# A fused attention and channel-mix kernel whose written-out order is replaced, with the drawn numbers packed one unit to a partition and the last output cut 384 and 128

## The chip, the core and the metric

One core of one Trainium2 chip runs the whole kernel. Its engines are TensorE (PE; its weight loads are shown apart as PEld), VectorE (DVE), ScalarE (ACT) and GpSimd (POOL); SyncE (SP) issues every DMA of this kernel. Each engine takes its instructions in the order in which they were written. The metric is device microseconds of one execution, as the median of timed runs. The profile is one further execution.

## The reference

```python
def _attn_ref(q, k, v, sampled_blocks):
    B, H, S, D = q.shape                      # 4, 8, 768, 64
    block = 32
    n_blocks = S // block                     # 24
    scores = 1.0 / np.sqrt(D) * np.matmul(q, k.transpose(0, 1, 3, 2))
    # kept: neighbours within one block, the first and the last block (as row and as column),
    # and three drawn blocks for each block of rows
    ...
    for qb in range(n_blocks):
        for kb in sampled_blocks[qb]:
            mask[qb * block:(qb + 1) * block, kb * block:(kb + 1) * block] = True
    scores = np.where(mask, scores, -1000000000.0)
    attn = np.exp(scores - np.max(scores, axis=-1, keepdims=True))
    attn = attn / (np.sum(attn, axis=-1, keepdims=True) + 1e-09)
    return np.matmul(attn, v)

def _moe_ref(x, mu_k, mu_r, w_k, w_v, w_r):   # x is the attention's output, 4 x 768 x 512
    x_prev = np.concatenate([np.zeros((B, 1, D)), x[:, :-1, :]], axis=1)
    xk = mu_k * x + (1.0 - mu_k) * x_prev
    xr = mu_r * x + (1.0 - mu_r) * x_prev
    k = np.maximum(xk @ w_k, 0.0)             # 512 to 1024
    v = k * k @ w_v                           # 1024 to 512
    r = 1.0 / (1.0 + np.exp(-(xr @ w_r)))
    return r * v
```

The weights come as float64; queries, keys and values as float32.

## The kernel before, in words

The attention is cut into 26 units. Units u0 to u21 each hold one block of 32 rows of all four batches; block n of unit u(n-1) looks at eight blocks of keys: itself, its two neighbours, the first, the last and three drawn ones. Units u22 to u25 hold the first and the last block of one batch, which look at all keys. Of a unit, two halves of `scores` (PE, line 402; tile `s`) are followed by `top` (DVE, the row maximum), `less` and four `exp` on ACT, a transposition (up to u3 on PE as `turn` and a copy `turned`; from u4 on DVE with a DMA called `move`), `values` (PE, lines 436 and 475; tile `o`), a division on DVE, and a copy into the mixer's input (`turn x`, `put x`).

The mixer works on tiles of 256 rows in the order 1 to 10, 0, 11. Tile t needs three units of attention. It computes `xr` and `xk` (mixes of x with its shifted self, each split into a high and a low part), two gates `r{t}_0` and `r{t}_1` (line 716), four pairs of hidden products `h{t}_0` to `h{t}_3` (line 737) and the outputs `v{t}_i` (line 772). Every product is three matmuls of fp32r parts. DVE multiplies gate and output, and SP stores them.

The twenty weights (w0 to w3 of the gate, w4 to w11 of the hidden products, w12 to w19 of the outputs) are loaded raw (512 KB each, `raw`) and turned into the two fp32r parts by six operations each: `size` on ACT, `tail`, `sign` and `lo` on one of two or three engines, `join` on DVE and `hi` on ACT or POOL. `CHOICE` says which engine.

Keys sit in twelve slots of the tile `KA`, values in `VA`. The slot for the neighbour key of a unit is the one that the unit before has last read: `u5 keys` can be issued by SP only when both `scores` of u4 have ended, and whatever stands behind it on SP waits with it. Which blocks were drawn is known only at run time: `pack` on DVE puts six drawn numbers of a unit into one word of the tile `packed`, SP loads a word of it (`TENSOR_LOAD`, line 266) ahead of a unit's first drawn load and takes the block numbers out by shifts.

All 2139 operations are written into a list, and a table of numbers, `ORDER`, says in which order they are emitted; an engine executes its own operations in that order. 128 small matmuls called `warm` come first on PE.

Of the kernel before, what the change touches and what calls it, by code (L numbers as in the profile page):

```python
# [95 lines left out]
def block_sparse_attention_channel_mix(  # L96
# [31 lines left out]
    packed = fixed([1, NEARS], I32, "packed")  # L128
# [3 lines left out]
    def mask_setup():  # L132
        pairs = NEARS * NRAND * SAME_AS
        drawn = buf([1, 2, pairs, 2], I32, "x0", 1, "drawn")
        e = buf([1, NEARS, NRAND, SAME_AS], F32, "x1", 1, "equal")
        r = buf([1, 6, NEARS, NRAND], F32, "kk", 3, "pickf")
        plan.add("drawn", SP, ISSUE, lambda: nc.sync.dma_start(drawn.ap.rearrange("p a b c -> p (a b c)"), blocks), writes=[(drawn,)], size=60000)

        def pack():
# [10 lines left out]
            half = r.ap[:, 2:4, :, 0]  # L150
            v.scalar_tensor_tensor(out=half, in0=both[:, :, :, 2], scalar=float(ROOM), in1=both[:, :, :, 1], op0=ALU.mult, op1=ALU.add)
            v.scalar_tensor_tensor(out=half, in0=half, scalar=float(ROOM), in1=both[:, :, :, 0], op0=ALU.mult, op1=ALU.add)
            whole = r.ap[:, 4:6, :, 0].bitcast(I32)
# [609 lines left out]
    def values(t, i, k2, z, last):  # L763
        final = t == TILES[-1] and i == 1
        width = DM // 2 if final else DM
        for n in range(0, DM, width):
# [3 lines left out]
            def mm(f, pv=pv, cs=cs):  # L770
# [224 lines left out]
```

## Time and profile before

| what | value |
| --- | --- |
| median of three timed runs | 520.68 us (516.51 to 520.86) |
| profiled execution, its own time | 519.15 us |
| its span, first to last instruction | 517.4 us |
| PE busy | 487.2 us (94%) |
| DVE, ACT, POOL busy | 321.1, 306.3, 207.1 us (62, 59, 40%) |
| mean granted clock of TensorE | 0.97 |
| bytes moved by DMA | 114.65 MB |

A busy share is an average over the whole span; which engine sets the pace has to be read stage by stage. The profiled execution lies 1.75 us above its span and 1.53 us under the median of the timed runs.

### The profile page before, as it was taken

How to read it: one execution, taken by the hardware profiler on the slowest of the kernel's cores; microseconds unless marked ns; L12 is line 12 of the kernel's file. 1: busy time of each engine (PE TensorE's matmuls, PEld its weight loads, DVE VectorE, ACT ScalarE, POOL GpSimd, SP SyncE). 2: the span in 40 equal slices, each digit the busy share in tenths (PEclk: the TensorE clock that was granted, in tenths of full speed). 3: DMA queues.
4: the chain of work that ended last, by engine and by line, in shares of the span. 5: the costliest groups of instructions: out<-in, count | busy, mean ns of one | idle time of the engine just before them, and what ended most of it. 6: DMA issues, size and time to landing. Idle time of an engine off the chain costs nothing.

```text
span 517.4 us, 18098 instructions
## 1 busy us (share of the span) xinstructions
PE 487.2 (94%) x7384; PEld 402.9 (78%) x7384; DVE 321.1 (62%) x608; ACT 306.3 (59%) x701; POOL 207.1 (40%) x253
## 2 busy tenths in 40 slices
PE   4568798999999999999999999999999999999997
PEld 4245587778779888878778878868778879889896
DVE  3667797976775865765665766763765653434231
ACT  2886887875736755546664745664646564445441
POOL 2425454352611722253452442233543525434531
PEclk8678899999999999999999999999999999999999
DMA  8999999988978888888898889999669553100101
GB/s 267 383 336 303 347 312 300 294 237 227 287 240 260 253 224 253 224 275 224 228 270 231 256 248 263 278 261 355 201 144 315 161 135 86 38 22 20 42 22 41
DMA packets 58052, 114.65 MB, mean 222 GB/s; under 512 B 7665, under 2 KB 20721, under 8 KB 55026
## 3 DMA queue, kind: packets, MB, share of 16 engines
q1 hardware_dynamic: 57970, 113.50, 72.1%
q8 instruction: 58, 0.95, 0.8%
q14 instruction: 24, 0.20, 0.1%
HBM read 77.82 MB, written 6.29 MB: 163 GB/s over the span
## 4 chain that ended last, share of the span: by engine, by line
PE 68%; DMA 11%; SPq 8%; DVE 4%; issue 4%; ACT 2%; POOL 2%; DVEq 0%; POOLq 0%; ACTq 0%
PE v L772 18%; PE s L402 7%; PE h_0p L737 6%; PE h_1p L737 6%; PE r_0p L716 6%; PE h_2p L737 6%; PE h_3p L737 5%; PE r_1p L716 5%; DMA KA<-kt 4%; PE o L475 4%; PE o L538 2%; DMA KA<-kq 2%; SPq L463 2%; PE sw L496 2%; DMA pt<-r 2%
## 5 line engine op out<-in xcount | busy, mean ns | idle before, releaser
L772 PE MATMUL v<-w,k 128*128 128x512 f32 (+1 forms) x600 | 138.9, 385 | 0.0
L772 PEld LDWEIGHTS v<-w,k 128*128 128x128 f32 x600 | 107.9, 188 | 26.7 <-issue 5.0
L412 DVE TENSOR_REDUCE nm<-s 128x4 f32<-128x1024 f32 x44 | 53.0, 1214 | 18.6 <-PE s L402 17.5
L402 PE MATMUL s<-KA,q 64*32 64x256 f32 x1408 | 51.9, 428 | 12.9 <-DMA raw<-w_k 9.9
L452 ACT ACTIVATE p<-s,nm 128x256 f32<-128x256 f32 x144 | 60.7, 479 | 0.6
L402 PEld LDWEIGHTS s<-KA,q 64*32 64x32 f32 x1408 | 28.1, 118 | 29.3 <-issue 10.6
L455 DVE STREAM_TRANSPOSE r<-p 128x1024 f32<-128x1024 f32 x36 | 43.5, 1227 | 9.7 <-ACT p L452 8.0
L475 PEld LDWEIGHTS o<-VA,pt 128*32 128x32 f32 x2304 | 34.0, 109 | 7.7 <-issue 4.1
L475 PE MATMUL o<-VA,pt 128*32 128x65 f32 x2304 | 37.4, 221 | 1.9 <-DMA pt<-r 1.1
L737 PE MATMUL h_2p<-xk,w 128*128 128x256 f32 x288 | 38.1, 285 | 0.2 <-ACT h_0k L752 0.2
L737 PEld LDWEIGHTS h_2p<-xk,w 128*128 128x128 f32 x288 | 36.0, 192 | 2.3 <-issue 1.2
L737 PEld LDWEIGHTS h_0p<-xk,w 128*128 128x128 f32 x288 | 35.6, 189 | 2.5 <-issue 1.0
L737 PEld LDWEIGHTS h_3p<-xk,w 128*128 128x128 f32 x288 | 35.6, 190 | 2.4 <-issue 1.2
L737 PE MATMUL h_3p<-xk,w 128*128 128x256 f32 x288 | 37.4, 285 | 0.0
L737 PE MATMUL h_0p<-xk,w 128*128 128x256 f32 x288 | 37.0, 282 | 0.4 <-DVE z L778 0.4
L716 PE MATMUL r_1p<-w,xr 128*128 128x512 f32 x144 | 37.2, 399 | 0.0
L737 PE MATMUL h_1p<-xk,w 128*128 128x256 f32 x288 | 37.1, 283 | 0.0
L737 PEld LDWEIGHTS h_1p<-xk,w 128*128 128x128 f32 x288 | 35.3, 189 | 1.5 <-issue 0.8
L716 PE MATMUL r_0p<-w,xr 128*128 128x512 f32 x144 | 36.5, 399 | 0.0
L666 ACT ACTIVATE xr_0d<-xt,mk 128x128 f32<-128x128 f32 x48 | 19.3, 402 | 21.3 <-DVE xr_0f L673 15.2
L716 PEld LDWEIGHTS r_0p<-w,xr 128*128 128x128 f32 x144 | 26.2, 188 | 6.7 <-issue 0.8
L416 ACT ACTIVATE nm<-nm 128x4 f32<-128x4 f32 x44 | 8.9, 202 | 36.1 <-DVE nm L412 36.0
(237 smaller groups left out, 837.7 us busy)
## 6 DMA issues: line engine op xcount, KB each, us to landing
VA<-vt SPq DMA_DIRECT2D x92, 260.0 KB, 4.5
KA<-kt SPq DMA_DIRECT2D x89, 256.0 KB, 4.3
pt<-r SPq DMA_DIRECT2D x72, 256.0 KB, 4.9
VA<-vw SPq DMA_DIRECT2D x24, 260.0 KB, 5.4
KA<-kq SPq DMA_DIRECT2D x16, 384.0 KB, 5.5
ptw<-rw SPq DMA_DIRECT2D x32, 192.0 KB, 3.6
out<-z SPq DMA_DIRECT2D x23, 256.0 KB, 3.7
q<-qt SPq DMA_DIRECT2D x22, 256.0 KB, 4.5
```

What stands on the lines that cost most here:

```text
L402: nc.tensor.matmul(s.ap[ROWS[j], row, a * 256 : (a + 1) * 256].rearrange("p (n x) -> p n x", x=BLK), q.ap[half, (hp * QB + j) * BLK : (hp ...
L412: nc.vector.tensor_reduce(out=nm.ap.rearrange("p (r a) -> p r a", r=2), in_=s.ap.rearrange("p r (a x) -> p r a x", a=2), axis=AX.X, op=ALU ...
L452: plan.add(f"u{name} exp {i}", ACT, 365, lambda row=row, a=a, i=i: nc.scalar.activation(squares()[:, :, :, i, :], s.ap[:, row, a * 256 : ( ...
L455: plan.add(f"u{name} turn", DVE, N_TURN, lambda: nc.vector.transpose(out=r.ap[:, :, gi].rearrange("p j c i x -> p j (c i x)"), in_=squares ...
L463: nc.sync.dma_start(pt.ap[:, b].rearrange("p g c i x -> p (g c i x)"), r.ap[ROWS[b]].rearrange("p j g c i x -> p j (g c i x)"))
L475: nc.tensor.matmul(o[gi].ap[ROWS[j], i * DV : (i + 1) * DV], pt.ap[:, j, gi, g, 2 * row + a, :], VA.ap[:, c0 + g, j, h * DV : (h + 1) * DV ...
L496: nc.tensor.matmul(s.ap[HALF[a], row, 0:W], q.ap[half, 2 * hp * BLK : 2 * (hp + 1) * BLK], wide_keys(b, hp)[half, k * W : (k + 1) * W], st ...
L538: nc.tensor.matmul(o.ap[ROWS[2 * a + e], c * DV : (c + 1) * DV], pt.ap[:, 2 * a + e, row, n, :], VA.ap[:, c1, part, h * DV : (h + 1) * DV] ...
L666: nc.scalar.activation(parts(d.ap), cols(c, 0), AF.Copy, scale=mk.ap[:, which, c : c + 1])
L716: nc.tensor.matmul(pr.ap[:, 0:512], xr.ap[:, a, c, :], weight_of["r", c].ap[:, w, :], start=(c == 0 and m == 0), stop=(c == CC - 1 and m = ...
L737: nc.tensor.matmul(ph.ap[:, ff * TT : (ff + 1) * TT], weight_of["k", c, f2 // 2].ap[:, w, f % 4 * P : (f % 4 + 1) * P], xk.ap[:, a, c, :], ...
L772: nc.tensor.matmul(pv.ap[:, 0:width], k2.ap[:, a, f, i * P : (i + 1) * P], weight_of["v", f].ap[:, w, cs], start=(f == 0 and m == 0), stop ...
```

## The change

Four edits are made.

1. `pack` works on 22 partitions, one unit each, in place of one partition: nine instructions as before, each over 1/22 of the elements. The drawn numbers are loaded as 22 rows of 336 bytes, and SP reads the word of a unit from that unit's partition.
2. The last output of the last tile, 512 columns, was computed in two parts of 256 columns; now in one of 384 and one of 128.
3. `ORDER` is replaced, and with it `CHOICE`: 18 in place of 14 `put x` of the attention's units run on ACT, 27 in place of 22 `hi` of xr on POOL, 23 in place of 16 `lo` of xr on DVE, and some others move one for one.
4. `warm` can take a data type. Its choice stays number 6, 128 matmuls of 64 bf16 columns, so the instructions of it stay.

```diff
-    packed = fixed([1, NEARS], I32, "packed")
+    packed = fixed([NEARS, 1], I32, "packed")
...
-        drawn = buf([1, 2, pairs, 2], I32, "x0", 1, "drawn")
-        e = buf([1, NEARS, NRAND, SAME_AS], F32, "x1", 1, "equal")
-        r = buf([1, 6, NEARS, NRAND], F32, "kk", 3, "pickf")
+        drawn = buf([NEARS, 2, NRAND * SAME_AS, 2], I32, "x0", 1, "drawn")
+        e = buf([NEARS, NRAND, SAME_AS], F32, "x1", 1, "equal")
+        r = buf([NEARS, 6, NRAND], F32, "kk", 3, "pickf")
...
-            sampled[n, by] = by.value_load(packed.ap[0:1, n - 1 : n], min_val=0, max_val=ROOM ** (2 * NRAND) - 1)
+            sampled[n, by] = by.value_load(packed.ap[n - 1 : n, 0:1], min_val=0, max_val=ROOM ** (2 * NRAND) - 1)
...
         final = t == TILES[-1] and i == 1
-        width = DM // 2 if final else DM
-        for n in range(0, DM, width):
+        for n, width in ((0, 384), (384, 128)) if final else ((0, DM),):
             pv = bank(f"v{t}_{i}_{n}", last)
...
 ORDER = [
-    0, 1, 2, 7, 16, 3, 11, 994, 973, 924, 14, 931, 4, 5, 13, 12, 10, 15, 926, 927, 925, 55, 966, 928, 933, 934, 56, 932, 974, 935, 996, 936, 6, 8, 995, 18, 937, 929, 997, 53,
+    3, 4, 1001, 1002, 14, 1004, 0, 7, 8, 11, 931, 1, 2, 12, 1003, 1005, 933, 13, 55, 1006, 1007, 10, 15, 16, 34, 973, 974, 975, 35, 5, 938, 36, 56, 934, 976, 977, 22, 932,
```

What the new numbers mean is seen in the order of an engine's instructions. In the rows below, `raw12` is the raw weight w12, `q5` the queries of u5, and the number behind an underscore counts buffers. SP, from the program's start, before:

```order
L159 DMA mk_70<-mu_r 128x4
L137 DMA drawn_207<-blocks 1x1848
L284 DMA KA_67<-kt 128x512
L187 DMA raw11_210<-w_k 128x1024
L187 DMA raw8_212<-w_k 128x1024
L187 DMA raw1_214<-w_r 128x1024
L284 DMA KA_67<-kt 128x512
L187 DMA raw2_217<-w_r 128x1024
L159 DMA mk_70<-mu_k 128x4
L284 DMA KA_67<-kt 128x2x512
L305 DMA q0_233<-qt 128x512
L266 TENSOR_LOAD packed_69
```

And after:

```order
L136 DMA drawn_207<-blocks 22x84
L186 DMA raw12_84<-w_v 128x1024
L283 DMA KA_67<-kt 128x512
L158 DMA mk_70<-mu_r 128x4
L283 DMA KA_67<-kt 128x512
L186 DMA raw2_98<-w_r 128x1024
L283 DMA KA_67<-kt 128x2x512
L304 DMA q0_240<-qt 128x512
L265 TENSOR_LOAD packed_69
```

Ahead of the drawn keys of u0, the last loads that u0's scores need, four weights stood, and two stand now.

SP further on, from u4's neighbour key (the first row of each) to u5's (the last); "..." stands for further rows of the same load and for register operations. Before:

```order
L284 DMA KA_67<-kt 128x512
...
L349 DMA VA_68<-vt 32x2080
...
L297 DMA VA_68<-vt 32x2080
L187 DMA raw12_1008<-w_v 128x1024
L305 DMA q5_1017<-qt 128x512
...
L332 DMA KA_67<-kt 128x512
...
L284 DMA KA_67<-kt 128x512
```

And after:

```order
L283 DMA KA_67<-kt 128x512
L186 DMA raw16_873<-w_v 128x1024
L186 DMA raw6_879<-w_k 128x1024
...
L348 DMA VA_68<-vt 32x2080
...
L296 DMA VA_68<-vt 32x2080
L186 DMA raw7_966<-w_k 128x1024
L304 DMA q5_994<-qt 128x512
...
L331 DMA KA_67<-kt 128x512
...
L283 DMA KA_67<-kt 128x512
```

Three drawn values (of u3) stood between the two keys, and six (of u3 and of u4) stand now; one weight stood there, and three stand now.

ACT, from its first instruction to the first `less` (L416, later L415) of u0. Lines 201, 215, 225 and 242 (later 200, 214, 224 and 241) are `size`, `tail`, `sign` and `hi` of weights. Before, without the row of the table load and of the first ACTIVATE:

```order
L215 ACTIVATE wf1_247<-raw1_214 128x512
L201 ACTIVATE wmag1_250<-raw1_214 128x512
L225 ACTIVATE wf2_256<-raw2_217 128x512
L201 ACTIVATE wmag2_271<-raw2_217 128x512
L201 ACTIVATE wmag8_273<-raw8_212 128x512
L242 CAST w2_278<-wf2_256 128x512
L201 ACTIVATE wmag11_282<-raw11_210 128x512
L242 CAST w1_286<-wf1_247 128x512
L225 ACTIVATE wf11_276<-raw11_210 128x512
L215 ACTIVATE wf8_309<-raw8_212 128x512
...
L416 ACTIVATE nm0_1_334<-nm0_1_334 128x4
```

And after:

```order
L200 ACTIVATE wmag12_86<-raw12_84 128x512
L224 ACTIVATE wf12_89<-raw12_84 128x512
L809 ACTIVATE mk_70<-const-float32-1.0 128x1
L214 ACTIVATE wf12_89<-raw12_84 128x512
L200 ACTIVATE wmag8_274<-raw8_272 128x512
L415 ACTIVATE nm0_1_278<-nm0_1_278 128x4
```

Twelve operations on weights (the dots leave out two, of w7) stood ahead of u0's first exponentials on ACT, and four stand now. Counted in the same way up to the last exponential of u2 they were 28 and are 19, up to that of u4 they were 31 and are 31.

## Rows read from the trace of the kernel before

**Rows 1.** Busy time of each engine, granted clock and DMA in four stretches.
```profile
core 0: us, PE busy (x) PEld busy (x) DVE busy (x) ACT busy (x) POOL busy (x), PEclk, DMA share, GB/s
...
17.06:60.34 43.28, 32.17 (x713) 20.73 (x713) 33.36 (x62) 34.78 (x84) 19.00 (x19) 0.81 0.96 344
60.34:110.20 49.86, 47.98 (x821) 38.03 (x821) 41.40 (x76) 39.50 (x89) 23.25 (x30) 0.93 0.90 284
110.20:514.40 404.20, 400.68 (x5725) 337.75 (x5724) 240.31 (x457) 225.24 (x520) 158.87 (x195) 1.00 0.68 199
514.40:517.40 3.00, 0.00 (x0) 0.00 (x0) 0.40 (x1) 0.00 (x0) 0.00 (x0) 1.00 0.13 44
```

**Rows 2.** What PE waited for: total us, times, longest.
```profile
PE s L402 <- DMA raw<-w_k: 9.9, 1, 9.9
PE s L402 <- DMA KA<-kt: 3.0, 3, 1.9
```

**Rows 3.** Timeline of PE: start, us, instructions, idle time before them.
```profile
17.06 3.29 PE L402 MATMUL s<-KA,q 64*32 64x256 f32 x64 [9.88 <-DMA raw<-w_k]
...
55.08 0.66 PE L371 MATMUL t3 0 1_960<-ident,p 128*128 128x128 f32 x4
55.57 0.68 PE L371 MATMUL t3 0 0_975<-ident,p 128*128 128x128 f32 x4
...
60.34 2.12 PE L402 MATMUL s<-KA,q 64*32 64x256 f32 x32 [0.99 <-DMA KA<-kt]
...
69.15 2.01 PE L402 MATMUL s<-KA,q 64*32 64x256 f32 x64
...
87.65 3.32 PE L402 MATMUL s<-KA,q 64*32 64x256 f32 x64 [1.88 <-DMA KA<-kt]
...
102.56 1.96 PE L402 MATMUL s<-KA,q 64*32 64x256 f32 x64
```

**Rows 4.** Windows on the DMA queue: last two numbers are share and GB/s.
```profile
0.00:7.00 7.00, 6.23 (x128) 6.26 (x128) 3.05 (x9) 1.49 (x2) 3.07 (x8) 1.00 0.63 166
7.00:64.00 57.00, 36.01 (x770) 22.77 (x774) 37.93 (x70) 41.91 (x95) 24.09 (x25) 0.76 0.97 350
...
64.00:66.00 2.00, 2.00 (x97) 1.32 (x82) 1.00 (x1) 1.36 (x5) 0.00 (x0) 0.95 0.15 58
...
10.00:11.00 1.00, 0.00 (x0) 0.00 (x0) 0.09 (x1) 0.09 (x1) 0.00 (x0) 0.50 1.03 388
```

**Rows 5.** SP: two issues in its timeline, and its longest wait in total.
```profile
6.16 0.64 SPq L305 DMA_DIRECT2D q<-qt  x1
...
64.99 0.34 SPq L284 DMA_DIRECT2D KA<-kt  x1
SPq L284 <- PE s L402: 7.7, 3, 3.3
```

**Rows 6.** Timeline of DVE: first and last of the nine instructions of `pack`.
```profile
2.88 0.63 DVE L144 TENSOR_TENSOR equal<-drawn 1x462 f32<-1x462 int32 x1 [2.88 <-DMA drawn<-blocks]
...
5.99 0.18 DVE L155 SCALAR_TENSOR_TENSOR packed<-pickf 1x22 int32<-1x22 int32 x1
```

**Rows 7.** A weight operation on ACT: busy us, mean ns of one, idle before.
```profile
L201 ACT ACTIVATE wmag<-raw 128x512 f32<-128x512 f32 x20 | 13.2, 666 | 0.7 <-DMA raw<-w_k 0.7
```

**Rows 8.** Late pieces of the chain that ended last: 24 matmuls of 256 columns, 12 of 512.
```profile
426.37 2.84 PE h_0p L737 x24
...
461.17 2.77 PE r_0p L716 x12
```

**Rows 9.** The end: DVE's last two outputs, and the store of 128 KB, us to landing.
```profile
511.51 0.69 DVE L778 SCALAR_TENSOR_TENSOR z<-v,z 128x512 f32<-128x512 f32 x1 [1.40 <-PE v L772]
514.38 0.42 DVE L778 SCALAR_TENSOR_TENSOR z<-v,z 128x256 f32<-128x256 f32 x1 [2.18 <-PE v L772]
out<-z SPq DMA_DIRECT2D x2, 128.0 KB, 1.7
```

More of the change, by code (lines that the diff above doesn't have):

```diff
@@ L142, in pack @@
             block, line, twice = (r.ap[:, i] for i in range(3))
-            one, other = (drawn.ap[:, i, :, 0].rearrange("p (n j m) -> p n j m", n=NEARS, j=NRAND) for i in range(2))
+            one, other = (drawn.ap[:, i, :, 0].rearrange("p (j m) -> p j m", j=NRAND) for i in range(2))
             v.tensor_tensor(out=e.ap, in0=one, in1=other, op=ALU.is_equal)
             v.tensor_reduce(out=twice, in_=e.ap, axis=AX.X, op=ALU.max)
-            v.tensor_copy(out=block, in_=one[:, :, :, 0])
+            v.tensor_copy(out=block, in_=one[:, :, 0])
             v.scalar_tensor_tensor(out=twice, in0=block, scalar=-float(NB), in1=twice, op0=ALU.add, op1=ALU.mult)
@@ L149, in pack @@
             both = r.ap[:, 0:2]
[L150 to L153, printed above, removed]
+            half = r.ap[:, 2:4, 0]
+            v.scalar_tensor_tensor(out=half, in0=both[:, :, 2], scalar=float(ROOM), in1=both[:, :, 1], op0=ALU.mult, op1=ALU.add)
+            v.scalar_tensor_tensor(out=half, in0=half, scalar=float(ROOM), in1=both[:, :, 0], op0=ALU.mult, op1=ALU.add)
+            whole = r.ap[:, 4:6, 0].bitcast(I32)
             v.tensor_copy(out=whole, in_=half)
-            v.scalar_tensor_tensor(out=packed.ap, in0=whole[:, 1], scalar=5 * NRAND, in1=whole[:, 0], op0=ALU.logical_shift_left, op1=ALU.bitwise_or)
-        plan.add("pack", DVE, 3550, pack, reads=[(drawn,)], writes=[(r,), (e,), (packed,)])
+            v.scalar_tensor_tensor(out=packed.ap, in0=whole[:, 1:2], scalar=5 * NRAND, in1=whole[:, 0:1], op0=ALU.logical_shift_left, op1=ALU.bitwise_or)
+        plan.add("pack", DVE, 1400, pack, reads=[(drawn,)], writes=[(r,), (e,), (packed,)])
         for w, m in enumerate((mu_k, mu_r)):
@@ L166, in warm, with run @@
         w = buf([P, 512], F32, "m", M_BUFS, "warm", ps)
-        def run(times, wide):
-            one = nc.const_aps.tensor(1.0, (P, 512), BF16)
+        def run(times, wide, dtype):
+            one = nc.const_aps.tensor(1.0, (P, 512), dtype)
             for i in range(times):
                 nc.tensor.matmul(w.ap[:, 0:wide], one[:, 0:P], one[:, 0:wide], start=(i == 0), stop=(i == times - 1))
-        choose("warm", [(PE, ns * many, 0, lambda many=many, wide=wide: run(many, wide)) for many, wide, ns in WARM],
-               writes=[(w,)], codes=[2 * many for many, wide, ns in WARM])
+        choose("warm", [(PE, ns * many, 0, lambda many=many, wide=wide, dtype=dtype: run(many, wide, dtype)) for many, wide, ns, dtype in WARM],
+               writes=[(w,)], codes=[(4 if dtype is F32 else 2) * many for many, wide, ns, dtype in WARM])
     weight_of = {}
@@ L764, in values, with mm @@
         final = t == TILES[-1] and i == 1
[L765 to L766 removed]
+        for n, width in ((0, 384), (384, 128)) if final else ((0, DM),):
             pv = bank(f"v{t}_{i}_{n}", last)
             cs = slice(n, n + width)
[L770 removed]
+            def mm(f, pv=pv, cs=cs, width=width):
                 for m, (a, w) in enumerate(TERMS):
@@ L777, in values @@
                          reads=[(k2, (0, f // 2), (1, f // 2)), (weight_of["v", f], 0, 1)], writes=[(pv,)], code=6)
-            plan.add(f"v{t}_{i}_{n} out", DVE, 75 + 1.05 * width, lambda pv=pv, cs=cs: nc.vector.scalar_tensor_tensor(
+            plan.add(f"v{t}_{i}_{n} out", DVE, 75 + 1.05 * width, lambda pv=pv, cs=cs, width=width: nc.vector.scalar_tensor_tensor(
                 out=z.ap[:, cs], in0=pv.ap[:, 0:width], scalar=unit, in1=z.ap[:, cs], op0=ALU.mult, op1=ALU.mult),
@@ L830 @@
 BANKS = [("m", M_BUFS)]
-WARM = [(20, 512, 219), (10, 512, 219), (1, 64, 60), (32, 64, 60), (64, 64, 60), (96, 64, 60), (128, 64, 60)]
+WARM = [(20, 512, 219, BF16), (10, 512, 219, BF16), (1, 64, 60, BF16), (32, 64, 60, BF16), (64, 64, 60, BF16), (96, 64, 60, BF16), (128, 64, 60, BF16),
+        (8, 512, 870, F32), (10, 512, 870, F32), (12, 512, 870, F32), (14, 512, 870, F32)]
 X_FROM = 6
@@ L977 @@
         "vw": con(con(vb).reshape(B, S // P, QB, BLK, HD).transpose(0, 1, 3, 2, 4)).reshape(B, S // P, P, HD),
-        "blocks": con(drawn).view(np.int32).reshape(1, -1),
+        "blocks": con(drawn.reshape(2, NEARS, -1).transpose(1, 0, 2)).view(np.int32).reshape(NEARS, -1),
         "mu_k": con(squares(inputs["moe_mu_k"]).reshape(CC, P).T),
```

1 line of the change is left out of this document (removed), and 184 rows, old and new, of tables (CHOICE, ORDER).

## The prediction

> **What bounds the kernel now.** I read the windows by stretch first, then PE's waits, then PE's and SP's timelines, then the windows on the DMA queue. The span falls into four parts [rows 1]. From 110.2 us on, PE is busy for 400.7 of 404.2 us at full clock: it is the bound, and 3.5 us are all that an order could win there. I went through PE's order from that point on in both programs: the same blocks follow one another, with neighbours swapped. So I price that part at no change. The end after PE, 3.0 us, is one product on DVE and one store. All the rest of PE's idle time lies ahead of 110.2 us: nearly 10 us before the first scores [rows 2, 3], 11 us from 17.1 to 60.3, 2 us from there to 110.2 [rows 1]; and in these parts the granted clock averages 0.81 and 0.93, the mean of stretches at either level.
>
> What ends the waits there is DMA. The scores of u0, u4 and u6 start when keys land [rows 2, 3], and from 7 to 64 us the queue has a share of 0.97 [rows 4]. The clock to read in this part is bytes: 1.16 MB moved by 7 us (166 GB/s times 7), then 350 GB/s on average, while a full queue moves 388 [rows 4]. The difference is holes, in which SP stood: it waited 7.7 us, in three places, for scores to end before it could issue a neighbour's key, 3.3 us of them before the issue at 64.99 [rows 5], and the queue was nearly empty at 64 to 66, with a share of 0.15 [rows 4].
>
> **The change part by part.** *First scores.* Up to the third drawn key of u0, SP issues before, in units of 256 KB: four of keys (one load is double), one of queries, three of drawn keys and eight for four weights, 16 units or 4.2 MB. Two weights less makes 3.15 MB. At 0.388 MB a us the first scores move by 1.05/0.388 = 2.7 us, from 17.06 to 14.4. A check of the clock: 7 us plus (4.2 - 1.16)/0.388 is 14.8, and the scores came at 17.06, so landing lags the byte clock by 2.2 us, which I use below.
>
> *Packing.* Its nine instructions take 2.88 to 6.17 us [rows 6], but SP came to the load of the packed word only behind the queries, at 6.80 [rows 5], so packing cost nothing where it stood. Now three issues fewer stand ahead, some 1.3 us, and the old form would come last by up to 0.7 us. Short instructions of it take 0.18 us [rows 6]; nine with the 0.05 us gaps make 2 us, and the numbers are SP's first load. So it stays hidden: 0, and at most 0.7 us to pay. That the word is read from another partition no row shows; I bound it by the spread between a wait hidden behind a full queue, 0, and 0.6 us, one issue [rows 5], and take 0.
>
> *ACT.* Up to the last exponential of u2, ACT has nine weight operations fewer ahead of it (28 to 19), 9 x 0.67 [rows 7] = 6 us of work in a stretch where it is busy for 34.8 of 43.3 us [rows 1]. Up to u4's last exponential the count is equal, so it is a loan until then: it lets scores of u1 to u3 end sooner, and with them the keys behind which SP stands. Taken alone it is worth 0 to 6 us at u3 and nothing at u5. Its worth shows in the queue, next.
>
> *The fifth unit.* Between u4's neighbour key and u5's, SP now issues two weights and three drawn values more, 1.05 + 3 x 0.27 = 1.85 MB, 4.8 us of a full queue. This is the price of the change. Counting everything that SP issues up to u5's neighbour key I get 21.3 MB before and 23.2 after. With the lag, u5's scores can start at 7 + (23.2 - 1.16)/0.388 + 2.2 = 66.0 us if the queue never runs dry, and at 7 + 22.04/0.350 + 2.2 = 72.2 us at the average rate of before. They started at 69.15 [rows 3]. Which of the two? At each point where SP has to stand for a score, more bytes lie ahead of it than before, and the scores come 2.7 us sooner or more: u2's key has 10.6 MB ahead (31 us by the full rate, and u1's scores should end near 27), u4's 18.2 MB (51 us, u3's scores ended at 52 and move by at least 2.7). So I place it by two thirds toward the full queue, at 68.0: -1.1 us. PE itself would be there near 65 (69.15 - 2.7 - 2, plus one gate product of 0.7 that now stands ahead of these scores), so a wait of some 3 us appears at u5.
>
> *The sixth unit.* Before, PE stood 1.88 us ahead of u6's scores, and these took 3.32 us in place of 1.96 [rows 3], at the lower clock. Between u5's key and the last load of u6 there are now two key loads' and one drawn unit's worth less on SP: 3.7 MB and one move of u4, some 11 us, against 16 us of PE work between the two scores. So the 1.88 us go; the 1.4 us of slow clock I leave, since the new pause at u5 can bring the same. With the gate product of 0.7 us that PE has already done: -2.6 us. Everything behind runs on PE alone, so what is won at u6 stays won: -1.1 - 2.6 = -3.7 us at 110.2.
>
> *The last output.* Before, 48 matmuls of 256 columns at 2.84/24 = 0.118 us [rows 8] are 5.68 us. 24 of 384 columns come, between 0.118 and 2.77/12 = 0.231 us [rows 8], to 0.175 us, 4.19 us in all. For 24 of 128 columns the line through both rows says 0.061 us, 1.47 us in all; but each has a weight load of its own, and the nearest row with 128 columns and a 128x128 load of four bytes is the transpositions, 0.49 us for four [rows 3], 0.122 each, 2.94 us in all. So the pair costs 5.66 to 7.13 us, 0 to +1.45. I take the upper end, since the weight load is the same. What follows gets shorter: DVE 0.42 to about 0.29 us by the line through its two rows, and a store of 64 KB in place of 128 KB (1.7 us [rows 9]) by up to 0.3 us; I take -0.3 in all. Together +1.1 us, bounds -0.4 and +1.3.
>
> The Trainium skill ("TensorE: Matmul & The Clock Gate", section "LDWEIGHTS (loading the stationary operand)") speaks against this edit: a load takes its columns divided by 1.2 GHz whatever the contraction, an estimate of 107 ns for 128. No run here shows a lone load; by it the 24 would take 2.6 us and the term would be +0.8.
>
> Edits without a price: the data type of `warm`, whose choice is the same; the line through which the drawn numbers are laid out in memory.
>
> Sum against the profiled execution: 519.15 - 3.7 + 1.1 = 516.5 us. That execution is 1.5 us under the median of the timed runs, which I leave: 516.5 is 0.8% under the median.
>
> **The rivals.** *The queue stays full and PE does not cool.* u5's scores start at 66.0 (-3.1), the wait at u6 goes with its slow clock (-0.7 - 1.88 - 1.4), the last output costs nothing (-0.4): 519.15 - 7.5 = 511.7. For it: the bytes ahead of each stand. Against it: PE would have to wait less than at u6 before, and the ACT loan would have to come through whole.
>
> *The head start is given back at u5.* The queue keeps 350 GB/s, u5 starts at 72.2 (+3.0), u6 gains 2.6, the end costs 1.1: 520.7, no change. For it: the rate is what was measured over 57 us. This is also the case in which the new order does not do what it says, a start that is early and an end that is not.
>
> *Slower: SP's holes grow.* SP takes everything in order, and two of its stands are now in front of longer rows of loads. If the ACT loan fails and two stands of 3.3 us as at 64.99 [rows 5] fall ahead of u5 in place of one, u5 starts at 72.2 + 3.3 = 75.5, +6.4; u6 gives 2.6 back, a long pause keeps the lower clock for another 1.4, the end costs 1.1: 525.4. It decides from the point at which the queue's average over 7 to 64 us falls under 330 GB/s. Against it: the first scores come earlier, and no row shows a reason for a second stand.
>
> **How the numbers follow.** The forecast (u5 between 66.5 and 70, 514 to 519) gets 0.47, the full queue 0.23, the gain given back 0.22, slower 0.08. The range takes the first three and part of the last, with the bounds of the end and 1 us for what the 3.5 us behind 110.2 may do: 511 to 522.5. Runs of this kernel differ by 0.8%, so 1% (515.5 to 525.9 around the median) is about what a measurement can tell. Under 515.5 lie the full queue and a third of the forecast, 0.39; above 525.9 half of the slower case, 0.05; between them 0.56.
>
> **What would show it.** First scores near 14.4 us; a wait of PE for keys just ahead of u5's scores and none ahead of u6's; the queue at 370 GB/s or more from 7 to 64 us and no stretch with a share under 0.5 there; r2_0, the gate of the second tile, at 106.5 in place of 110.2; from there to PE's last matmul the same 404 us plus 1.4; the 24 last matmuls in 2.9 us. It is wrong if u6's scores still wait, if PE loses several us at a new place behind 110.2, or if first scores do not move.

## The result, and the profile after

The changed kernel took 520.02 us (median of 22 runs, 515.62 to 522.99), the kernel before in the same set 518.38 us (22 runs, 511.49 to 523.62). The ratio is 1.0056, 95% interval 1.0035 to 1.0078: by it 0.56% slower, where 0.8% faster was forecast. Runs more than 1.5% above the fastest of their kernel are left out of the ratio, and one run of 511.49 us takes 9 of the 22 of before out with it. Over all runs the medians differ by 0.3%, and a second set (e5 below) gave 1.0018 (0.9981 to 1.0055). So the size of the loss is open; but the gain of 0.8% did not come in either set.

The profiled execution of the changed kernel took 516.15 us, the second fastest of its 22. Read by itself against the 519.15 us of before, it would have confirmed the forecast to 0.4 us. That is the trap of this case: most of the difference between the two profiles is not the change.

Four stretches of the profile after, cut at the same events as in [rows 1]: first scores, u4's scores, r2_0, PE's end.

```profile
14.26:58.48 44.22, 32.24 (x712) 22.25 (x712) 34.39 (x68) 34.39 (x81) 15.78 (x15) 0.80 1.00 374
58.48:108.53 50.05, 47.35 (x822) 36.97 (x821) 45.26 (x76) 41.55 (x91) 28.34 (x33) 0.97 0.92 282
108.53:511.60 403.07, 398.48 (x5724) 336.66 (x5724) 240.02 (x455) 224.32 (x518) 160.39 (x204) 1.00 0.67 198
511.60:514.40 2.80, 0.04 (x1) 0.00 (x0) 0.29 (x1) 0.00 (x0) 0.00 (x0) 0.75 0.08 23
```

From u4's scores to r2_0 PE is busy for 47.35 of 50.05 us, DVE for 45.26, ACT for 41.55; before it was 47.98, 41.40 and 39.50 of 49.86. Whatever arrives early at u4's scores has to pass this stretch, in which PE and DVE are nearly full and ACT is not far from it. In the rows that follow, the name behind the arrow is what the profile takes to have ended the wait. What PE waited for up to 110 us, to be held against [rows 2]:

```profile
PE s L401 <- DMA KA<-kt: 7.8, 1, 7.8
PE t0 0 1_351 L370 <- ACT p L422: 4.7, 1, 4.7
PE o L435 <- DMA VA<-vt: 4.6, 3, 1.9
PE s L401 <- DVE xk1f L672: 2.2, 1, 2.2
```

PE's timeline after, the rows that answer to [rows 3]:

```profile
14.26 3.67 PE L401 MATMUL s<-KA,q 64*32 64x256 f32 x64 [7.79 <-DMA KA<-kt]
22.65 1.11 PE L370 MATMUL t0 0 1_351<-ident,p 128*128 128x128 f32 x4 [4.72 <-ACT p L422]
...
58.48 1.54 PE L401 MATMUL s<-KA,q 64*32 64x256 f32 x32
...
69.14 1.94 PE L401 MATMUL s<-KA,q 64*32 64x256 f32 x32 [2.23 <-DVE xk1f L672]
...
86.50 1.96 PE L401 MATMUL s<-KA,q 64*32 64x256 f32 x64
108.53 3.05 PE L715 MATMUL r_0p<-w,xr 128*128 128x512 f32 x12
```

The first scores come 2.8 us earlier (17.06 to 14.26). At u4 1.9 us of that are left (60.34 to 58.48), at u5 nothing (69.15 to 69.14), at u6 1.15 (87.65 to 86.50), at r2_0 1.7 (110.16 to 108.53). The new 4.72 us stand ahead of u0's first turn: in the new order ACT does two operations on w2 and one on w8 ahead of u0's first exponential, and one each on w3 and w1 among its eight. The four weight operations counted under "The change" are those up to u0's first `less`; with these three it is seven that stand ahead of the first exponential, against twelve.

The wait of 2.23 us ahead of u5's scores is put down to an operation of DVE on the mixer's `xk1f`, which the scores (`s<-KA,q`) do not read. The last key that they read is SP's issue at 62.50:

```profile
L283 SPq DMA_DIRECT2D KA<-kt x1: 1324/1324/1324, 62.5 to 62.5; - x1
DMA to landing us min/median/max: 6.3/6.3/6.3
```

It landed at 68.8, 0.3 us ahead of the scores, which began at 69.14: the wait was for the key. ([rows 3] has the like: a weight's load is named ahead of u0's scores.)

The queue did what was hoped of it. Its average over 7 to 64 us rose from 350 to 364 GB/s, and the hole at 64 to 66 us [rows 4] is gone (in the profiles below: 353 to 374 GB/s where the new order stands unaltered up to r2_0, 349 and 351 with the old one):

```profile
7.00:64.00 57.00, 37.76 (x799) 25.56 (x802) 42.10 (x77) 39.52 (x94) 23.18 (x25) 0.82 0.98 364
64.00:66.00 2.00, 2.00 (x129) 1.91 (x123) 1.90 (x2) 2.00 (x6) 2.00 (x2) 1.00 1.04 396
```

SP's wait for scores fell from 7.7 us [rows 5] to 3.9 (`SPq L283 <- PE s L401: 3.9, 3, 2.4`). The nine instructions of `pack` end at 3.78 us where they ended at 6.17 [rows 6]:

```profile
2.22 0.17 DVE L143 TENSOR_TENSOR equal<-drawn 22x21 f32<-22x21 int32 x1 [2.22 <-DMA drawn<-blocks]
...
3.63 0.15 DVE L154 SCALAR_TENSOR_TENSOR packed<-pickf 22x1 int32<-22x1 int32 x1
```

SP issues its first drawn keys at 5.64 us, so packing is hidden by 1.9 us. At the end, the rows that answer to [rows 9]:

```profile
509.05 0.69 DVE L776 SCALAR_TENSOR_TENSOR z<-v,z 128x512 f32<-128x512 f32 x1 [2.82 <-PE v L770]
511.67 0.29 DVE L776 SCALAR_TENSOR_TENSOR z<-v,z 128x128 f32<-128x128 f32 x1 [1.94 <-PE v L770]
```

Between the starts of these two DVE steps lie exactly the last 24 matmuls, now of 128 columns: 2.62 us. Before it was 514.38 - 511.51 = 2.87 us for 24 of 256 [rows 9]. Half the columns save 9%.

### The profile page after: what moved, and what is told of

Same layout as the page of the kernel before. It is cut to its first block, busy times and chain, and to the rows that moved or that the text cites. A ratio compares the mean times of both kernels' runs of the same rounds, so it can differ in the third digit from the quotient of the medians.

```text
span 514.4 us, 18084 instructions
## 1 busy us (share of the span) xinstructions
PE 483.8 (94%) x7384; PEld 401.5 (78%) x7384; DVE 324.8 (63%) x611; ACT 303.6 (59%) x694; POOL 209.2 (41%) x262
## 4 chain that ended last, share of the span: by engine, by line
PE 69%; SPq 9%; DMA 7%; DVE 6%; ACT 4%; issue 3%; POOL 1%; DVEq 0%; POOLq 0%; ACTq 0%
PE v L770 21%; PE h_1p L736 6%; PE s L401 6%; PE h_3p L736 6%; PE h_0p L736 6%; PE o L474 5%; PE r_0p L715 5%; PE h_2p L736 5%; PE r_1p L715 4%; SPq L462 3%; DMA VA<-vt 3%; PE o L537 2%; PE sw L495 2%; DVE nm L411 2%; DMA KA<-kt 2%
## 5 line engine op out<-in xcount | busy, mean ns | idle before, releaser
L770 PE MATMUL v<-w,k 128*128 128x512 f32 (+2 forms) x600 | 139.7, 387 | 0.0
L770 PEld LDWEIGHTS v<-w,k 128*128 128x128 f32 x600 | 109.1, 188 | 26.8 <-issue 3.9
L401 PE MATMUL s<-KA,q 64*32 64x256 f32 x1408 | 49.5, 405 | 12.2 <-DMA KA<-kt 7.8
L401 PEld LDWEIGHTS s<-KA,q 64*32 64x32 f32 x1408 | 26.6, 112 | 26.9 <-issue 14.3
L736 PE MATMUL h_2p<-xk,w 128*128 128x256 f32 x288 | 36.2, 280 | 0.1
L736 PEld LDWEIGHTS h_2p<-xk,w 128*128 128x128 f32 x288 | 34.6, 188 | 0.9 <-issue 0.4
L665 ACT ACTIVATE xr_1d<-xt,mk 128x128 f32<-128x128 f32 x48 | 19.4, 403 | 22.0 <-POOL xr_1f L669 12.7
```

The costliest lines, as they stand in the source:

```text
L401: nc.tensor.matmul(s.ap[ROWS[j], row, a * 256 : (a + 1) * 256].rearrange("p (n x) -> p n x", x=BLK), q.ap[half, (hp * QB + j) * BLK : (hp ...
L665: nc.scalar.activation(parts(d.ap), cols(c, 0), AF.Copy, scale=mk.ap[:, which, c : c + 1])
L736: nc.tensor.matmul(ph.ap[:, ff * TT : (ff + 1) * TT], weight_of["k", c, f2 // 2].ap[:, w, f % 4 * P : (f % 4 + 1) * P], xk.ap[:, a, c, :], ...
L770: nc.tensor.matmul(pv.ap[:, 0:width], k2.ap[:, a, f, i * P : (i + 1) * P], weight_of["v", f].ap[:, w, cs], start=(f == 0 and m == 0), stop ...
```

## Experiments

Each was timed in 12 runs against the kernel before on the same chip. The intervals are wide (about 0.3% either way), so the starts in the traces carry more than the times. "Order" is the list by which the operations are issued; edits to it are shown by the names of operations.

**e1_tail256: the old columns in the changed kernel.**

```diff
-        for n, width in ((0, 384), (384, 128)) if final else ((0, DM),):
+        for n, width in ((0, 256), (256, 256)) if final else ((0, DM),):
```

> The changed kernel with one edit taken back: the last output in 256 and 256 columns as before; order and packing stay new. The changed kernel was measured at 1.0056 of the kernel before (+2.9 us). If the narrow last matmuls carry a good part of that (theory TAIL: 24 matmuls of 128 columns at about 0.11 us and 24 of 384 at 0.175, 6.8 us, against 5.68 for 48 of 256, less 0.3 us at the very end), this kernel is 0.8 us faster than the changed one, ratio to before about 1.004. If the loss lies in the order alone (theory ORDER), it stays at 1.0056. In its profile the 48 last matmuls of 256 columns should take 5.7 us, and the way from the end of the last matmul to the end of the span 3.0 us.

517.79 us, ratio 0.9991 (0.9963 to 1.0019). Its DVE rows at the end:

```profile
513.19 0.69 DVE L776 SCALAR_TENSOR_TENSOR z<-v,z 128x512 f32<-128x512 f32 x1 [2.76 <-PE v L770]
516.05 0.42 DVE L776 SCALAR_TENSOR_TENSOR z<-v,z 128x256 f32<-128x256 f32 x1 [2.17 <-PE v L770]
```

Behind r11_1's last gate product PE has 51 matmuls left in both kernels, 15 of 512 columns, 12 of the first narrow piece and 24 of the second, then comes the last DVE step: 8.37 us after (503.30 to 511.67) and 7.92 here (508.13 to 516.05). So 12 of 384 columns take 0.45 + 0.24 = 0.69 us more than 12 of 256, and 24 of them 1.38; the 24 of 128 give 0.24 back. That is +1.14 us on PE. Behind PE, from the last DVE step to the end of the span, it is 2.73 instead of 3.05 us. The new columns cost 0.8 us by the trace. The time missed what either theory said: both started from 1.0056, which e5 below does not repeat, and expected 1.004 or more. It has the sign of TAIL, but is too wide for the size.

**e2_old_order: the old order with the new packing and columns.**

```diff
-CHOICE, ORDER = new
+CHOICE, ORDER = old
```

> The changed kernel with the order and the engine choices of the kernel before: what is left of the change is the packing on 22 partitions and the 384 and 128 columns. TAIL: +0.8 us, ratio about 1.0015, and the packing nothing; ORDER then accounts for the other +2.1 us. If the packing or the columns carried everything, the ratio would be 1.0056. If the new order gains 3.7 us as forecast and the small edits lose it, it would be over 1.01.

520.20 us, ratio 0.9997 (0.9961 to 1.0033). The interval holds +0.15%, and nothing as large as +1% or +0.56%; but the plain medians of the set are 520.20 and 518.19 us, 0.4% apart, so only +1% is safely out. Of use is the trace: it is the old order in another execution, and shows what of [rows 3] was the order and what was that execution. The wait of 1.88 us ahead of u6's scores, on which the forecast built its largest term, is not there:

```profile
69.02 1.93 PE L401 MATMUL s<-KA,q 64*32 64x256 f32 x56
72.64 0.64 PE L401 MATMUL s<-KA,q 64*32 64x256 f32 x8 [1.69 <-issue]
...
87.73 0.83 PE L401 MATMUL s<-KA,q 64*32 64x256 f32 x17
88.88 1.53 PE L401 MATMUL s<-KA,q 64*32 64x256 f32 x47 [0.31 <-issue]
```

And yet u6's scores come at 87.73, as in [rows 3] (87.65): here PE stood for 1.69 us within u5's scores, for a reason that the profile does not give ("issue"). r2_0 comes at 109.34.

**e3_newfront and e4_newback: one order up to r2_0, the other behind it.**

```diff
 e3  ORDER = new up to "r2_0 0" + what is left, as old has it
 e4  ORDER = old up to "r2_0 0" + what is left, as new has it
```

> New order and engine choices up to the first matmul of r2_0, from there on the old ones; packing and columns new. If the front carries the loss (theory FRONT: the 4.7 us wait for u0's exps and the earlier weight loads, which in most executions cost more than the profiled one showed), the ratio is that of the changed kernel, 1.0056. If the part behind r2_0 carries it (theory BACK: PE idle 4.6 us instead of 3.5 there, and more in other executions), this kernel is faster than the changed one by 1 to 3 us; and if the front gains 1.7 us, as the two single profiles say, the ratio is about 0.998.

> Old order up to the first matmul of r2_0, from there on the new one; packing and columns new. FRONT: the old front takes the loss away, ratio about 1.0015 (the columns alone). BACK: the loss stays, ratio 1.004 to 1.009, with PE idle of 4 us and more behind r2_0. r2_0 should start near 110 us, as in the kernel before.

e3: 518.57 us, ratio 1.0017 (0.9983 to 1.0052). e4: 519.58 us, 1.0036 (1.0005 to 1.0066). They don't tell front from back: either part may carry nothing or 1 to 2 us. In the traces r2_0 came at 111.63 with the new front and at 107.63 with the old one, the reverse of the two profiles that I had compared. The rows of e4, u6 and r2_0:

```profile
85.48 0.83 PE L401 MATMUL s<-KA,q 64*32 64x256 f32 x17
87.16 1.53 PE L401 MATMUL s<-KA,q 64*32 64x256 f32 x47 [0.86 <-issue]
...
107.63 3.05 PE L715 MATMUL r_0p<-w,xr 128*128 128x512 f32 x12
```

PE did not stand ahead of u6's scores in this execution of the old front, and these came 17.0 us behind u5's in place of 18.5. So 1.5 us were won here without the new order, and r2_0 came earlier than in any profile of this case with the new front. That set the next question: how far apart are two executions of one program?

**e5_again: the changed kernel, unchanged.** There is no edit.

> The changed kernel itself once more, unchanged, as the control of this set and for a second profile of it. In the first profile (an execution of 516.15 us, the second fastest of 22) r2_0 began at 108.5 us and 392.0 us lay from there to the first matmul of r11_1; the same instructions in the kernel with the old columns took 109.1 and 396.1. If the executions differ by themselves (theory SPREAD), this profile lies elsewhere again, by 1 us or more in either stretch. If the profiled execution was typical, it shows 108.5 and 392 within 0.5 us. Time: 519 to 520 us median.

517.84 us, ratio 1.0018 (0.9981 to 1.0055). r2_0 came at 108.42 (108.53 in the first profile), and 392.75 us lay from there to r11_1 (391.99). So this pair agrees better than theory SPREAD wanted; the median lies below the 519 to 520 us expected. But e1 has the same instructions up to the last output, and there the stretch took 396.06 us; in e9 and e11 below, which share them too, 395.79 and 393.87. (Twelve matmuls of the last output stand in the stretch; with the old columns of e1 and e11 they make it 0.7 us shorter, not longer.) The spread is 4 us within one order, and e1 shows one place of it. First PE's timeline after, then that of e1, both from the same hidden product on:

```profile
155.73 1.52 PE L736 MATMUL h_0p<-xk,w 128*128 128x256 f32 x12
157.35 1.96 PE L401 MATMUL s<-KA,q 64*32 64x256 f32 x64
159.24 1.66 PE L736 MATMUL h_0p<-xk,w 128*128 128x256 f32 x12
```

```profile
156.47 1.52 PE L736 MATMUL h_0p<-xk,w 128*128 128x256 f32 x12
160.26 3.58 PE L401 MATMUL s<-KA,q 64*32 64x256 f32 x64 [2.27 <-issue]
163.77 1.71 PE L736 MATMUL h_0p<-xk,w 128*128 128x256 f32 x12
```

In e1 a set of scores began 2.27 us late and then took 3.58 us in place of 1.96, at a granted clock of 0.83 over 160 to 170 us where the other had 1.00. From this hidden product to the next it is 7.30 us against 3.51: one late start cost 3.8 of the 4.1 us between the two executions. The profile gives nothing that ended the wait ("issue"), so what was late in e1 stays open. At the same place PE waited 1.21 us in e9 and 0.93 us in e11, both put down to ACT's `h_1k`; there the granted clock stayed at 1.00 and the scores took 1.96 us.

**e6_exps: u0's exponentials ahead of the weights on ACT.**

```diff
 ACT  u0 1 less
-     w2 sign, w2 size, w8 hi, u0 0 less, u0 0 exp 3, u0 1 exp 2, 1, 3, w3 size, u0 0 exp 2, 1, 0, w1 size, u0 1 exp 0
+     u0 1 exp 0, 1, 2, 3, u0 0 less, u0 0 exp 3, 2, 1, 0, u0 1 0 turned, u0 1 1 turned, w8 hi, w2 sign, w2 size, w3 size, w1 size
 PE   u0 1 scores, u0 0 scores
-     u0 0 1 turn, u1 1 scores, u0 1 0 turn, u0 1 1 turn
+     u0 1 0 turn, u0 1 1 turn, u0 0 1 turn, u1 1 scores
```

> The changed kernel with one piece of the order altered: u0's eight exps and the copies of its first two turns stand ahead of the three weight operations (w8 hi, w2 sign, w2 size) and w3 size on ACT, and PE turns u0's second half first. The first turn should start near 19.5 us instead of 22.65, and u1's scores near 21.5 instead of 23.70. Theory EXPS (that wait of 4.7 us is what gives the head start back): u4's, u5's and r2_0's starts come 2 us earlier too, r2_0 near 107. Theory QUEUE (the values and keys of u1 to u5 come out of the full queue at a time of their own): the 2 us are waited for again at u1's and u2's values, u5's scores stay at 68.5 to 72 and r2_0 at 108.5 or later; time within 0.5 us of the control.

520.46 us, ratio 1.0065 (1.0030 to 1.0100). PE's timeline:

```profile
18.18 0.80 PE L370 MATMUL t0 1 0_322<-ident,p 128*128 128x128 f32 x4 [0.41 <-ACT p L422]
...
22.04 1.12 PE L370 MATMUL t0 0 1_367<-ident,p 128*128 128x128 f32 x4 [2.33 <-ACT pt L374]
23.09 2.99 PE L401 MATMUL s<-KA,q 64*32 64x256 f32 x64
```

The first turn came 4 us earlier than in the control, at 18.18. The third then waited 2.33 us for ACT's copies of the first two (`pt`), and u1's scores started at 23.09, no sooner than in the control (23.22). u4's came at 60.72 and r2_0 at 110.89, 2 us later than in the control, which is within the spread of the new front; the median lies 2.6 us above the control's. The gain of EXPS did not come. But the wait was only moved, from the first turn to the third, so the run does not say what an earlier u1 would be worth. QUEUE had the first part right (no gain) and not the second (a loss of 2.6 us); why it is a loss is not shown.

**e7_queue: 1.84 MB moved behind u5's keys.**

```diff
 SP   u2 values 1 1
-     w13, u4 q, u4 keys 4, w16, w6, u3 drawn values, u4 drawn values, u3 values 1 2, w7, u5 q, u5 drawn keys, u5 keys 5, u6 q
+     u4 q, u4 keys 4, w6, u3 drawn values, u3 values 1 2, w7, u5 q, u5 drawn keys, u5 keys 5, u6 q, u4 drawn values, w16, w13
 ACT  w13 size and w16 size behind u5's scores
```

> The changed kernel with u4's drawn values and the loads of w16 and w13 moved behind u6's q on the queue (where the kernel before has the drawn values and w16), and these two weights' first ACT operation behind u5's scores: 1.84 MB less ahead of u5's keys. QUEUE: 1.84 MB at 0.364 MB/us are 5 us, of which PE can use the 2.2 us that it waits: u5's scores near 67 instead of 69.1, r2_0 near 106.5, time about 2 us below the control. EXPS: u5's scores no earlier than 68.5, time within 0.5 us of the control.

518.94 us, ratio 1.0018 (0.9984 to 1.0053), as the control. PE's timeline in the control (e5) and then here:

```profile
67.88 1.10 PE L401 MATMUL s<-KA,q 64*32 64x256 f32 x32 [1.24 <-ACT p L451]
68.91 1.09 PE L736 MATMUL h_3p<-xk,w 128*128 128x256 f32 x7
70.84 0.86 PE L736 MATMUL h_3p<-xk,w 128*128 128x256 f32 x5 [0.84 <-DVE xk L684]
...
86.24 1.96 PE L401 MATMUL s<-KA,q 64*32 64x256 f32 x64
```

```profile
66.48 1.09 PE L401 MATMUL s<-KA,q 64*32 64x256 f32 x32
67.50 0.97 PE L736 MATMUL h_3p<-xk,w 128*128 128x256 f32 x6
69.43 0.38 PE L736 MATMUL h_3p<-xk,w 128*128 128x256 f32 x1 [0.96 <-POOL xk L688]
70.77 1.43 PE L736 MATMUL h_3p<-xk,w 128*128 128x256 f32 x5 [0.95 <-DVE xk L684]
...
86.22 1.96 PE L401 MATMUL s<-KA,q 64*32 64x256 f32 x64
```

This is the run to learn from. u5's scores came 1.4 us earlier and waited for nothing, near the 67 that QUEUE expected. The next block, `h_3p`, then waited for its operand from POOL and DVE and went on at 70.77, where the control had 70.84; u6's scores came at 86.22 and 86.24, r2_0 at 108.72 and 108.42. The wait was not removed, it changed its owner. One pair of profiles could be chance, but e8 and e10 below carry the same edit and repeat it. From u4's scores to u5's it is 7.78 us in e7, 7.76 and 7.80 in these, without a wait, against 8.8 to 11.0 in the six profiles with the new front as it is; from u4's to u6's it is 27.5, 27.5 and 27.8 us, against 27.4 to 28.3.

**e8_both256: both edits, and the old columns.** The edits of e6, e7 and e1 together.

> Both edits of the order at once, and the last output in 256 and 256 columns again. QUEUE: as with the queue's edit alone and 0.8 us at the end besides, about 3 us below the control, and 1.5 to 2 us below the kernel before, if that lies 1 us below the control. EXPS: 2 us from the exps and 0.8 us at the end. If neither (the rest of the schedule is late on something else): 0.8 us below the control.

519.60 us, ratio 1.0044 (1.0010 to 1.0079); u4's scores at 62.02, r2_0 at 112.42. None of the three expectations came, not even the 0.8 us of the columns by the time. The profiled execution was the slowest of the 12 (524.34 us), so its front, 4 us later than the control's, says little by itself.

**e9_narrow64: the suspected cost of the tail doubled.**

```diff
-                    nc.tensor.matmul(pv.ap[:, 0:width], k2.ap[:, a, f, i * P : (i + 1) * P], weight_of["v", f].ap[:, w, cs],
-                                     start=(f == 0 and m == 0), stop=(f == FC - 1 and m == 2))
+                    each = 64 if width == 128 and f + m else width
+                    for x in range(0, width, each):
+                        nc.tensor.matmul(pv.ap[:, x : x + each], k2.ap[:, a, f, i * P : (i + 1) * P],
+                                         weight_of["v", f].ap[:, w, cs.start + x : cs.start + x + each], ...
```

> The changed kernel with the suspected cost of the tail doubled: 23 of the last 24 matmuls of 128 columns are issued as two of 64 each, over the same weights. TAIL, as a floor for each matmul (the weight load of about 0.11 us that comes with it sets the pace, not the columns): 23 more matmuls at 0.11 us, the way from the last 512-column DVE step to the last 128-column one grows from 2.62 us to about 5.1, and the time by 2.5 us above the control. If the columns alone set the time, it stays at 2.6 us and the time at that of the control.

520.99 us, ratio 1.0062 (1.0028 to 1.0095). DVE's last steps:

```profile
512.35 0.69 DVE L779 SCALAR_TENSOR_TENSOR z<-v,z 128x512 f32<-128x512 f32 x1 [2.82 <-PE v L772]
517.71 0.29 DVE L779 SCALAR_TENSOR_TENSOR z<-v,z 128x128 f32<-128x128 f32 x1 [4.67 <-PE v L772]
```

5.36 us for 47 matmuls is 0.114 us each, where 24 of 128 columns took 0.109 and 24 of 256 took 2.86/24 = 0.119. With a quarter of the columns a matmul of this kind is not faster: TAIL, a floor for each matmul, is shown. In the trace the matmuls have a weight load each, also where two in turn use the same weights (one or two records are missing):

```profile
L772 PE MATMUL v<-w,k 128*128 128x64 f32 x46 | 5.5, 281 | 0.0
L772 PEld LDWEIGHTS v<-w,k 128*128 128x128 f32 x45 | 5.3, 197 | 0.0
```

That the floor comes from this load of 128 columns, and not from a fixed cost of every matmul, fits the `values` of a unit, whose loads have 32 columns: 128 of them take 2.03 us, 0.016 each, in the changed kernel's profile (u4's, at 80.12 us). The median is 3.2 us above the control's, with the kernel before at 518.36 here and 518.24 there.

**e10_values256: the values of u1 and u2 pulled ahead**, on top of e7 and e1.

```diff
 SP   u1 drawn values
-     w14, u1 values 1 0, w10, u1 values 0 3, u3 drawn keys, u3 keys 6, w9, u3 q, w4, u4 drawn keys, u2 drawn values, u2 values 1 1
+     w5, u1 values 1 0, u1 values 0 3, w14, w10, u3 drawn keys, u3 keys 6, u2 drawn values, w9, u3 q, w4, u4 drawn keys, u2 values 1 1
```

> The changed kernel with columns 256 and 256, the queue's edit (u4's drawn values, w16 and w13 behind u6's q), and the queue between u0 and u2 turned: the loads of w14 and w10 behind u1's values, w5 behind u1's drawn values, u2's drawn values ahead of w9. Theory VALUES (the head start of the first scores is waited for at u1's and u2's values, 1.9 us and 1.9 to 2.8 us in the two profiles of the changed kernel, and from u4's scores on PE is nearly full, so r2_0 lies 50 us behind these): the waits for VA fall to 2 us in sum, u4's scores come at 56 to 57 instead of 58.5 to 59, r2_0 at 106 to 107, and the time is 1.5 to 2 us below the control. Rival WEIGHTS (what is pulled ahead pushes keys and weights back): u4's scores at 58.5 or later, r2_0 at 108.5 or later, time as the control's.

521.02 us, ratio 1.0055 (1.0021 to 1.0088). The waits for `VA` are gone from the list of PE's waits, as VALUES wanted, and others stand in it:

```profile
PE t1 0 1_630 L370 <- DVE pt L375: 3.8, 1, 3.8
PE o L435 <- issue: 1.9, 1, 1.9
```

u4's scores came at 61.92 (58.81 in e5, 60.32 in e11), r2_0 at 111.89 (108.42 and 110.43). The gain of VALUES did not come: as WEIGHTS said, something else is late now (here a copy on DVE, and SP stood for 11.0 us in place of 3.7 to wait for scores). What the values alone would be worth, with the rest on time, no run shows.

**e11_tail256b: e1 once more**, as the control of this set.

> The changed kernel with columns 256 and 256, once more, as the control of this set. TAIL: 0.8 us below the changed kernel, so within 0.3% of the kernel before if the order alone is worth nothing; r2_0 between 108.4 and 109.1 and 392 to 396 us from there to r11_1's first matmul, as in the profiles so far.

518.05 us, ratio 0.9989 (0.9950 to 1.0029). With e1, that is twice no difference to the kernel before that these intervals could show. r2_0 came at 110.43, 1.3 us outside what I expected: the front has a spread of its own.

**e12_xk256: the operand that was late in e7, made earlier**, on top of e7 and e1.

```diff
 DVE  xk1 mix 0, u4 0 top, xk1 mix 1, u4 1 top, xk1 lo 0, xk1 mix 3
-     w6 join, u4 0 turn, xk1 mix 2, u4 1 turn, xk1 lo 1
+     xk1 mix 2, w6 join, xk1 lo 1, u4 0 turn, u4 1 turn
 ACT  xk1 now 2 directly behind xk1 now 3;  POOL  xk1 hi 1 ahead of w4 lo
```

> The queue's edit again (u5's scores near 66.5), with columns 256 and 256, and on top of it the second half of xk1 pulled ahead of u4's two transposes: xk1 now 2 behind xk1 now 3 on ACT, xk1 mix 2, hi 1 and lo 1 before u4's first transpose on DVE and before w4 lo on POOL. With the queue's edit alone u5's first scores came 1.4 us earlier than in the control (66.48 against 67.88), but h1_3's matmuls then waited 0.96 us for POOL's xk and 0.95 us for DVE's, and went on at 70.77, as in the control (70.84). Theory DVE (xk1 comes out of DVE and POOL at its own time and is what is late next): that wait goes to under 0.3 us, h1_3 runs on at 68.5, u6's scores come at 84.5 to 85 and r2_0 at 106.5 to 107, 1.5 to 2 us below the queue's edit alone (108.72). Rival PE (or ACT) full: the transposes, now later, make u4's values or u5's turns late, u6's scores at 86 or later, r2_0 at 108.5 or later. Time: 1.5 us below the kernel with columns 256 and 256 by DVE, the same by the rival.

522.01 us against 520.32 for the kernel before on this chip, ratio 1.0037 (1.0005 to 1.0069). PE's timeline:

```profile
67.95 1.10 PE L401 MATMUL s<-KA,q 64*32 64x256 f32 x32 [1.88 <-ACT p L451]
68.97 2.79 PE L736 MATMUL h_3p<-xk,w 128*128 128x256 f32 x12
...
87.58 1.96 PE L401 MATMUL s<-KA,q 64*32 64x256 f32 x64
```

`h_3p` runs through without a wait. Now u5's scores wait, 1.88 us for ACT's exponentials of u4, which have ACT's part of xk1 ahead of them (u5's key had landed at 64.9); and u6's come 1.4 us later than in e7, r2_0 at 109.95. The rival was right: moved off DVE's turn, the wait stands at ACT.

## Why the forecast was wrong

The sum was -3.7 us at r2_0 and +1.1 us at the end. Measured: no gain at r2_0 that nine profiles can show, and +0.8 at the end. Three profiles have the old order up to r2_0 (before, e2, e4), six have the new one unaltered (after, e1, e3, e5, e9, e11). Mean starts in us (the differences are those of the unrounded means):

| start of | old | new | difference |
| --- | --- | --- | --- |
| u0's scores | 17.2 | 14.2 | -3.0 |
| u2's scores | 37.9 | 34.4 | -3.5 |
| u3's scores | 48.3 | 46.5 | -1.9 |
| u4's scores | 59.8 | 59.3 | -0.5 |
| u5's scores | 68.9 | 69.1 | +0.2 |
| u6's scores | 87.0 | 87.1 | +0.1 |
| r2_0 | 109.0 | 109.4 | +0.3 |

- **First scores, 14.4 us: right.** 14.26 in the first profile, 13.78 to 14.76 in the others with this front, by two weight loads fewer ahead. **Packing: right**, hidden by 1.9 us.
- **ACT's loan, "worth 0 to 6 us at u3 and nothing at u5"**: right in kind; the front is early at u2 and u3, in spite of the new wait of 4.72 us at u0. It is used up sooner than I thought: most of it between u2 and u4, where PE waits for values and copies. Which of these decides is not shown; e10, without the waits for values, did not gain.
- **u5's scores at 68.0, "-1.1 us": the mechanism right, the size not.** A wait for keys was to appear ahead of them, and it does, 0.6 to 3.1 us in the six profiles (3 had been forecast). In five of the six the profile puts it down to ACT or DVE, to three different operations; but in after, e1, e3 and e9 the key landed 0.3 to 0.4 us ahead of the scores (the landing in e5 and e11 is not in the trace). What was mis-sized is the queue: 68.0 needs some 375 GB/s from 7 us on, and the six profiles have 353 to 374 over 7 to 64 us, 364 on average. With 364 the forecast's own formula gives 69.7. In the kernel before, this formula at the measured 350 GB/s gives 66.7, not 69.15: there the key landed at 67.7 and PE came to these scores later, so they were not bound by bytes.
- **u6, "the 1.88 us go ... what is won at u6 stays won", -2.6 us: the step that failed.** It took the wait of one execution for a property of the order. Two more executions of the old front do without it: in e4 u6's scores then come 2.2 us earlier, in e2 a pause of 1.69 us at u5 takes its place. From u5's scores to u6's it is 18.0 us on average with the new front and 18.1 with the old: nothing where -2.6 had been summed. The sign that I had named for it, no wait ahead of u6's scores, came in all six; the gain did not. I had priced this stretch by PE and the queue alone. DVE is busy for 45.26 and ACT for 41.55 of its 50.05 us, and e7 and e12 show that an early key is followed by a wait for DVE and POOL, and with their part ahead, by one for ACT. From u4's scores to r2_0 the six profiles with the new front take 49.6 to 50.6 us, and e6, e7, e8 and e10, with their edits, 50.0 to 50.4; e12 takes 51.8. So what is left at u4, 0.5 us, is all that r2_0 could get, and it is lost in the spread.
- **r2_0 at 106.5: not reached in any run.** New front: 108.04 to 111.63; old front: 107.63 to 110.16. Both spread over 2.5 to 3.6 us, so a difference under 1.5 us can't be told from none.
- **Behind 110.2, "no change", and 1 us for it in the range: no change that can be shown, but too narrow.** Executions of the same instructions differ by 4 us between r2_0 and r11_1: 392.0 to 396.1 with the new order there, 394.9 to 398.8 with the old.
- **The last output, +1.1: mechanism right, size +0.8.** The 24 matmuls of 128 columns were priced by the transposition's 0.122 us each and took 0.109. The 384-column piece was priced at 4.19 us and took (2.86 + 1.38 =) 4.24; what follows PE became shorter by 0.32 us for the 0.3 estimated. The Trainium skill ("TensorE: Matmul & The Clock Gate", section "LDWEIGHTS (loading the stationary operand)") gave an estimate of 107 ns for a 128-column load, 2.6 us for the 24 and +0.8 for the term. The traces agree with it: 2.62 us here, and in e9 the same pace with half the columns.

The time that came is that of the rival "the head start is given back at u5", priced at 520.7 us with a chance of 0.22. That is luck: its terms did not come. u5's scores were to start at 72.2 and start at 69.1, u6 was to gain 2.6 us and gained nothing, and the queue was to stay at 350 GB/s and reached 364.

Shown by the runs: the columns cost 0.8 us, and the front's early start is used up before r2_0, most of it before u4. Open: whether the order by itself is worth anything within about 1 us (e1 and e11 together say 0.999, each with 0.3 to 0.4% either way), and whether the 2.9 us that the ratio of 1.0056 stands for hold anything but the columns' 0.8 us and the spread. The plain medians speak for little more: against the kernel before in the same set, the changed kernel is at +1.6 us (first set) and -0.4 (e5), the one with the old columns at -0.4 (e1) and -0.3 (e11). `ORDER` and `CHOICE` were never run apart, nor the packing without the columns.

## What to carry to other kernels

Before a wait is written down as a gain, ask for a second execution, and look whether the engines around it have room: here three engines were 83 to 95% busy over a stretch, and an earlier input only changed which one was waited for. Before the name in a wait is believed, look when the operand itself landed. A split into narrower last pieces should be priced by the number of matmuls, each with its weight load, and not by columns alone; what DVE and the store saved behind PE was about a quarter of what PE lost.

## What I had not expected of the hardware

One start that was 2.27 us late cost 3.8 us in the middle of the program (e1): at a granted clock of 0.83 over the ten microseconds from 160 us on, the mean of stretches at either level, 64 scores took 3.58 us in place of 1.96. Pauses of 1.21 and 0.93 us at the same place (e9, e11) left the clock at 1.00. Matmuls of 64, 128 and 256 columns with a fresh 128x128 load of four-byte weights took 0.114, 0.109 and 0.119 us each, that is, nearly the same (e9, after, e1); those of 384 took some 0.177.
